# Threshold mask of an attention stage as a steep Prelu and a scaled exponential on ScalarE, with minimum pass and f16 copy on VectorE

## Chip, cores and metric

One Trainium2 chip, one core. The metric is the device time of one execution in microseconds, the median over runs; smaller is better.

## The reference

Attention with a threshold mask over 4 batches, 8 heads, 576 positions and 64 dimensions, then two gated layers on the 2304 tokens:

```python
scores = scale * np.matmul(q, k.transpose(0, 1, 3, 2))
thresh = np.max(scores, axis=-1, keepdims=True) - tau
scores = np.where(scores >= thresh, scores, -1000000000.0)
scores = scores - np.max(scores, axis=-1, keepdims=True)
attn = np.exp(scores)
attn = attn / (np.sum(attn, axis=-1, keepdims=True) + 1e-09)
x = np.matmul(attn, v)                       # then heads side by side: 2304 x 512
x = (1 / (1 + np.exp(-(x @ w_gate))) * (x @ w_val)) @ w_out
x = ((x @ w1) * (x @ w2) @ w3) @ w_out2
```

Only scores within tau (0.02) of the maximum of their row keep a weight.

## The kernel before

**Slices.** Two heads of one batch form a pair; there are 16 pairs, four to a batch. A pair is worked in nine slices of 128 rows (four for each head, and one with the last 64 rows of both heads), 144 slices in all, numbered g. A slice's scores are 128 x 576 numbers of f32 in one of two PSUM buffers (ps_s0 and ps_s1, by g odd or even).

**One slice, before.** s_mm computes the scores on TensorE. s_max (L321) takes the negated row maximum on VectorE. s_exp (L327, L328) computes the exponential into an SBUF tile e, and the threshold as a 128 x 1 column, both on ScalarE. s_mask (L336) compares the scores with the threshold, multiplies e with the outcome and adds up the row sums, on VectorE; after it the PSUM buffer is free for slice g + 2. s_hi (L344) copies e, scaled by 16384, to f16 on ScalarE. s_lo makes the rest that f16 lost, as a second f16: in the first batch and in every even slice it rescales e in place (L355 on ScalarE in the first two batches, L357 on GpSimd later) and subtracts on GpSimd (L358); in the odd slices of the other three batches one VectorE instruction (L360) does both. s_tr transposes the pair of f16 tiles by a DMA on SyncE's queue, and pv multiplies with v on TensorE five slices later.

**Order.** Engines work their own queues in order. A loop over g writes all steps; the block of s_mask, s_max, s_exp and s_mm is marked as of high priority, and a scheduler sorts all instructions by readiness in a timeline of its own and by priority. Buffers: four tiles e, four f16 tiles, five transposed ones, three of each 128 x 1 column.

**Work between.** In the first batch, TensorE multiplies w3 with w_out2 between the slices (tiles ps, th, tl, woh, wol). Later it works on the first gated layer of the batch that is finished (tiles ps_h, ps_o; 36 of its 60 units before the attention ends). Weights come as 64-bit numbers and are converted on VectorE (L450, L456), ScalarE (L455) and GpSimd (L459), then split into a high and a low part on ScalarE (L468) and GpSimd or VectorE (L469). After the attention come the rest of the first layer and the second one.

Of the kernel before, what the change touches and what calls it, by code (L numbers as in the profile page):

```python
# [8 lines left out]
F32 = mybir.dt.float32  # L9
# [13 lines left out]
def kernel(  # L23
# [33 lines left out]
    NC = S // P  # L57
    TL = S - NC * P
    NKB = NC + 1
    PSC = 16384.0  # L60

    def mm(out_, lhsT, rhs, first, last):
        nc.tensor.matmul(out_, lhsT, rhs, start=first, stop=last)  # L63
# [1 line left out]
    cst = ctx.enter_context(tc.tile_pool(name="cst", bufs=1))  # L65
# [14 lines left out]
    taub = cst.tile([P, 1], F32, name="taub")  # L80
    nc.sync.dma_start(taub, tau.partition_broadcast(P))
    zq = cst.tile([P, 1], F32, name="zq")
    nc.vector.tensor_scalar(zq, taub, 0.0, float(D) ** -0.5, op0=ALU.is_ge, op1=ALU.mult)
    ntau = cst.tile([P, 1], F32, name="ntau")
    nc.vector.tensor_scalar(ntau, taub, -1.0, None, op0=ALU.mult)
    nc.vector.tensor_tensor(ntau, ntau, taub, op=ALU.min)

    XR = cst.tile([P, KC, NT], U32, name="XR")
    XA = XR.bitcast(F32)
# [2 lines left out]
    ap_ = actx.enter_context(tc.tile_pool(name="attn", bufs=1, side="right"))  # L92
# [35 lines left out]
    prep = {}  # L128
# [126 lines left out]
    def v_scale(pr):  # L255

        vx = ap_.tile([P, 1], F32, tag="vx", name="vx")
        nc.vector.reduce_max(vx, prep[pr]["vt"], axis=AX.X)
        vp = ap_.tile([P, 1], F32, tag="vp", name="vp")
        nc.vector.tensor_single_scalar(  # L260
            vp.bitcast(I32), vx.bitcast(I32), 0x7F800000, op=ALU.bitwise_and
        )
        nc.vector.tensor_scalar(vp, vp, 2.0 ** -96, 2.0 ** 125, op0=ALU.max, op1=ALU.min)
        vs = ap_.tile([P, 1], F32, tag="vs", name="vs")
        nc.vector.reciprocal(vs, vp)
        vi = ap_.tile([P, 1], F32, tag="vi", name="vi", bufs=3)
        nc.vector.tensor_scalar(vi, vp, 1.0 / (8192.0 * PSC), None, op0=ALU.mult)
        vb = ap_.tile([P, P], BF16, tag="vb", name="vb")
        nc.scalar.activation(vb, vs.to_broadcast([P, P]), AF.Copy, scale=8192.0)
        prep[pr].update(vb=vb, vi=vi)  # L270
# [21 lines left out]
    st = {}  # L292
    NSL = 2 * NC + 1
# [22 lines left out]

    def s_max(g):
        x = st[g]
        nm = ap_.tile([P, 1], F32, tag="nm", name="nm", bufs=3)
        th = ap_.tile([P, 1], F32, tag="th", name="th", bufs=3)  # L320
        nc.vector.tensor_reduce(nm, x["ps"], axis=AX.X, op=ALU.max, negate=True)  # L321
        x.update(nm=nm, th=th)

    def s_exp(g):
        x = st[g]
        e = ap_.tile([P, S], F32, tag="e", name="e", bufs=4)
        nc.scalar.activation(e, x["ps"], AF.Exp, bias=x["nm"])  # L327
        nc.scalar.activation(x["th"], x["nm"], AF.Identity, scale=-1.0, bias=ntau)  # L328
        x["e"] = e

    def s_mask(g):
        pr, s = divmod(g, NSL)
        x = st[g]
        if s == 0:
            prep[pr]["sum"] = ap_.tile([P, NSL], F32, tag="sum", name="sum", bufs=2)
        nc.vector.scalar_tensor_tensor(  # L336
            x["e"], x["ps"], x["th"], x["e"], op0=ALU.is_ge, op1=ALU.mult,
            accum_out=prep[pr]["sum"][:, s:s + 1],
        )

    def s_hi(g):
        x = st[g]
        x["h16"] = ap_.tile([P, 2 * S], F16, tag="h16", name="h16", bufs=4)
        nc.scalar.activation(  # L344
            x["h16"][:, 0:S], x["e"], AF.Copy, scale=PSC
        )

    def s_lo(g):
        e = st[g]["e"]
        hb = st[g]["h16"]  # L350
        hi, lo = hb[:, 0:S], hb[:, S:2 * S]
        b = g // (NPAIR * NSL)
        if b == 0 or g % 2 == 0:
            if b < 2:
                nc.scalar.activation(e, e, AF.Copy, scale=PSC)  # L355
            else:
                nc.gpsimd.tensor_scalar(e, e, PSC, 1.0, op0=ALU.mult, op1=ALU.mult)  # L357
            nc.gpsimd.tensor_tensor(lo, e, hi, op=ALU.subtract)  # L358
        else:
            nc.vector.scalar_tensor_tensor(lo, e, PSC, hi, op0=ALU.mult, op1=ALU.subtract)  # L360

    def s_tr(g):
        pt = ap_.tile([P, 2 * NC + 1, P], F16, tag="pt", name="pt", bufs=5)
# [21 lines left out]
    def x_norm(pr):  # L385
        p = prep[pr]
        rs = ap_.tile([P, NSL], F32, tag="rs", name="rs", bufs=1)
        nc.vector.tensor_scalar(rs, p["sum"], 1e-9, None, op0=ALU.add)
        nc.vector.reciprocal(rs, rs)
        xn = ap_.tile([P, NC, 2, D], F32, tag="xn", name="xn")  # L390
        xt = ap_.tile([P, 2, D], F32, tag="xt", name="xt")
        nc.vector.tensor_tensor(
            xn.rearrange("p c h d -> p h c d"), p["u"],
            rs[:, 0:2 * NC].rearrange("p (h c x) -> p h c x", h=2, x=1).to_broadcast([P, 2, NC, D]),
            op=ALU.mult,
        )
# [384 lines left out]
    G = NP * NSL  # L781
# [83 lines left out]
    for g in range(G + LAG + 3):  # L865
        pr, s = divmod(g, NSL)
        steps = ahead[s] if pr + 1 < NP else ([],) * 5
        done = divmod(g - LAG, NSL)
        with tc.high_priority(offset=RING):
            if g < G:  # L870
                s_mask(g)
            if g + 1 < G:
                s_max(g + 1)
                s_exp(g + 1)
            if g + 2 < G:
                s_mm(g + 2)
# [12 lines left out]
        for f in steps[0]:
            f(pr + 1)  # L890
        for f in steps[1]:
            f(pr + 1)
        if done[1] == 2 and done[0] > 0:
            x_act(done[0] - 1)
            if done[0] % NPAIR == 0:
                xdone[0] = done[0] // NPAIR
        filler(g, 0)
        for f in steps[2]:
            if isinstance(f, str):
                if pr + 2 < NP:  # L900
# [280 lines left out]
```

## Time and profile before

| | us |
|---|---|
| median of 3 runs | 1119.43 (1118.0 to 1125.42) |
| span of the profiled execution | 1115.6 |
| TensorE (matmul) busy | 1008.3, 90% |
| VectorE busy | 774.8, 69% |
| ScalarE busy | 627.6, 56% |
| GpSimd busy | 676.3, 61% |

PE is TensorE, PEld its weight load, DVE VectorE, ACT ScalarE, POOL GpSimd, SP SyncE. L12 is line 12 of the kernel. Shares of busy time are means over stages with different limits: attention with work between it until some 673 us, gated layers afterwards. A busy TensorE is not TensorE at its peak, and the granted clock (PEclk, as a share of full speed) differs between stretches.

### The profile page before, as it was taken

Reading aid. Unit: us, or ns where it says so; the run is one execution under the profiler, and the core shown is the slowest. Engines: PE = TensorE matmul, PEld = TensorE weight load, DVE = VectorE, ACT = ScalarE, POOL = GpSimd, SP = SyncE. Lnnn points to the kernel's source line nnn. Section 1 sums busy time; section 2 is a strip of 40 time slices with the busy share of each in tenths; the row PEclk is TensorE's granted clock in tenths of the full one; section 3 lists DMA queues with packets and bytes.
Section 4 is the critical chain, followed back from the end, with each engine's and each line's share of the span. In section 5 each row is a group of like instructions: output and inputs, shape, how many; then the busy total and the mean of one; then the engine's idle time right before and its main releaser. Section 6 shows DMA issues by size and latency. Waiting matters only on the chain. (4 is left out here: it accounts for less than half of the span.)

```text
span 1115.6 us, 20323 instructions
## 1 busy us (share of the span) xinstructions
PE 1008.3 (90%) x6960; PEld 884.9 (79%) x6960; DVE 774.8 (69%) x1380; ACT 627.6 (56%) x1245; POOL 676.3 (61%) x577
## 2 busy tenths in 40 slices
PE   2598956898987999999999998999999999999997
PEld 2477845676765787777877888999999989988996
DVE  6978687888897767767877645776767644652741
ACT  4868898767777676567667644554442322331321
POOL 3755475587888586678677855677664643462530
PEclk9789967999988999999999999999999999999999
DMA  8999999999999999898988864677558826844922
GB/s 227 245 274 211 225 218 173 241 280 264 270 286 235 200 209 210 211 210 180 201 198 184 161 140 153 215 234 250 184 193 293 256 80 229 282 131 128 325 69 63
DMA packets 322422, 232.57 MB, mean 208 GB/s; under 512 B 225296, under 2 KB 253968, under 8 KB 322320
## 3 DMA queue, kind: packets, MB, share of 16 engines
q1 hardware_dynamic: 322320, 231.28, 80.9%
q8 instruction: 55, 0.90, 0.3%
q14 instruction: 47, 0.39, 0.1%
HBM read 133.17 MB, written 30.93 MB: 147 GB/s over the span
## 5 line engine op out<-in xcount | busy, mean ns | idle before, releaser
L358 POOL TENSOR_TENSOR h<-e,h 128x576 f16<-128x576 f32 x90 | 120.1, 1336 | 39.9 <-ACT e L355 29.7
L327 ACT ACTIVATE e<-ps_s,nm 128x576 f32<-128x576 f32 x144 | 106.1, 737 | 51.0 <-DVE nm L321 49.8
L336 DVE SCALAR_TENSOR_TENSOR e<-ps_s,th,e 128x576 f32<-128x576 f32 x144 | 116.2, 811 | 20.3 <-ACT th L328 12.5
L63 PEld LDWEIGHTS <-pt 128*128 128x128 f16 x2240 | 82.1, 101 | 58.8 <-DMA pt<-h 32.3
L321 DVE TENSOR_REDUCE nm<-ps_s 128x1 f32<-128x576 f32 x144 | 106.3, 751 | 28.9 <-PE ps_s L63 19.9
L344 ACT ACTIVATE h<-e 128x576 f16<-128x576 f32 x144 | 97.0, 678 | 28.3 <-DVE e L336 14.8
L63 PE MATMUL ps_s<-ka,qa 128*128 128x288 f32 x256 | 67.5, 351 | 42.2 <-DVE e L336 31.4
L63 PE MATMUL ps_h<-xl,gh 128*128 128x512 f32 (+1 forms) x240 | 94.7, 395 | 6.3 <-POOL xl L469 2.8
L63 PE MATMUL ps_h<-xl,vh 128*128 128x512 f32 (+1 forms) x240 | 92.7, 386 | 2.4 <-ACT th L685 1.3
L63 PE MATMUL ps_h<-xh,gl 128*128 128x512 f32 (+1 forms) x240 | 91.3, 380 | 3.3 <-POOL gl L469 3.3
L469 POOL TENSOR_TENSOR gl<-wg,gh 128x512 fp32r<-128x512 f32 x42 | 55.4, 1319 | 61.4 <-ACT gh L468 61.4
L63 PE MATMUL ps_y<-wm,abh 128*128 128x512 f32 x288 | 91.6, 390 | 0.2 <-DVE wm L469 0.2
L63 PE MATMUL ps_h<-xh,vl 128*128 128x512 f32 (+1 forms) x240 | 90.2, 376 | 1.6 <-POOL vl L469 1.6
L63 PE MATMUL ps_o<-gvl,oh 128*128 128x512 f32 (+1 forms) x240 | 90.4, 376 | 1.0 <-DVE XR L718 1.0
L63 PE MATMUL ps_h<-xh,gh 128*128 128x512 f32 (+1 forms) x240 | 90.8, 378 | 0.0
L63 PE MATMUL ps_h<-xh,vh 128*128 128x512 f32 (+1 forms) x240 | 90.2, 376 | 0.0
L63 PE MATMUL ps_o<-gvh,ol 128*128 128x512 f32 (+1 forms) x240 | 88.5, 369 | 0.3 <-POOL ol L469 0.3
L63 PE MATMUL ps_o<-gvh,oh 128*128 128x512 f32 (+1 forms) x240 | 88.2, 368 | 0.0
L63 PE MATMUL u<-vh,pt 128*128 128x64 f16 x640 | 62.6, 200 | 27.6 <-DMA pt<-h 27.2
L63 PEld LDWEIGHTS ps_s<-ka,qa 128*128 128x128 f32 x256 | 45.6, 210 | 50.5 <-DVE e L336 36.5
L360 DVE SCALAR_TENSOR_TENSOR h<-e,h 128x576 f16<-128x576 f32 x54 | 61.4, 1137 | 23.2 <-ACT h L344 22.8
L469 POOL TENSOR_TENSOR ol<-wo,oh 128x512 fp32r<-128x512 f32 x42 | 55.7, 1330 | 24.0 <-ACT oh L468 23.9
(198 smaller groups left out, 3025.2 us busy)
## 6 DMA issues: line engine op xcount, KB each, us to landing
wc<-sc_c SPq DMA_DIRECT2D x168, 256.0 KB, 3.2
sc_c<-wc SPq DMA_DIRECT2D x56, 256.0 KB, 2.9
XR<-in_moe_w_out_dram SPq DMA_DIRECT2D x20, 512.0 KB, 5.0
ka<-xk SPq DMA_DIRECT2D x64, 144.0 KB, 3.3
wg<-sc_g SPq DMA_DIRECT2D x36, 256.0 KB, 3.1
wv<-sc_v SPq DMA_DIRECT2D x36, 256.0 KB, 3.1
wo<-sc_o SPq DMA_DIRECT2D x36, 256.0 KB, 3.2
XR<-in_moe_w_dram SPq DMA_DIRECT2D x16, 512.0 KB, 5.0
```

Source lines behind the costliest of these rows:

```text
L63: nc.tensor.matmul(out_, lhsT, rhs, start=first, stop=last)
L321: nc.vector.tensor_reduce(nm, x["ps"], axis=AX.X, op=ALU.max, negate=True)
L327: nc.scalar.activation(e, x["ps"], AF.Exp, bias=x["nm"])
L336: nc.vector.scalar_tensor_tensor(x["e"], x["ps"], x["th"], x["e"], op0=ALU.is_ge, op1=ALU.mult, accum_out=prep[pr]["sum"][:, s:s + 1],)
L344: nc.scalar.activation(x["h16"][:, 0:S], x["e"], AF.Copy, scale=PSC)
L358: nc.gpsimd.tensor_tensor(lo, e, hi, op=ALU.subtract)
L360: nc.vector.scalar_tensor_tensor(lo, e, PSC, hi, op0=ALU.mult, op1=ALU.subtract)
L469: (lo_eng or nc.gpsimd).tensor_tensor(lo, x, hi.bitcast(F32), op=ALU.subtract)
```

## The change

q is now scaled by the negative factor, so that PSUM holds negated scores. s_max is one VectorE instruction that adds |tau| to them and accumulates the row minimum (nt, the negated threshold); its full output goes to the tile e and is overwritten later. s_exp is two ScalarE instructions: Prelu in place in PSUM, which turns the scores into score minus threshold and multiplies negative ones by 2^126, and an exponential with a bias that brings in the factor 1024 and accumulates the row sums into sum. s_mask is gone, and with it the threshold column and the rescalings. s_hi is a VectorE copy (it appears as CAST), s_lo one subtraction, on VectorE for every third slice of the last three batches (36) and on GpSimd otherwise (108). s_mm of slice g + 2 is written ahead of s_max and s_exp of slice g + 1.

```diff
-    nc.vector.tensor_scalar(zq, taub, 0.0, float(D) ** -0.5, op0=ALU.is_ge, op1=ALU.mult)
+    nc.vector.tensor_scalar(zq, taub, 0.0, -float(D) ** -0.5, op0=ALU.is_ge, op1=ALU.mult)
...
     def s_max(g):
         x = st[g]
-        nm = ap_.tile([P, 1], F32, tag="nm", name="nm", bufs=3)
-        th = ap_.tile([P, 1], F32, tag="th", name="th", bufs=3)
-        nc.vector.tensor_reduce(nm, x["ps"], axis=AX.X, op=ALU.max, negate=True)
-        x.update(nm=nm, th=th)
+        nt = ap_.tile([P, 1], F32, tag="nt", name="nt", bufs=3)
+        e = ap_.tile([P, S], F32, tag="e", name="e", bufs=4)
+        nc.vector.tensor_scalar(e, x["ps"], tauc, None, op0=ALU.add, op1=ALU.min, accum_out=nt)
+        x.update(nt=nt, e=e)
 
     def s_exp(g):
-        x = st[g]
-        e = ap_.tile([P, S], F32, tag="e", name="e", bufs=4)
-        nc.scalar.activation(e, x["ps"], AF.Exp, bias=x["nm"])
-        nc.scalar.activation(x["th"], x["nm"], AF.Identity, scale=-1.0, bias=ntau)
-        x["e"] = e
-
-    def s_mask(g):
         pr, s = divmod(g, NSL)
         x = st[g]
         if s == 0:
             prep[pr]["sum"] = ap_.tile([P, NSL], F32, tag="sum", name="sum", bufs=2)
-        nc.vector.scalar_tensor_tensor(
-            x["e"], x["ps"], x["th"], x["e"], op0=ALU.is_ge, op1=ALU.mult,
-            accum_out=prep[pr]["sum"][:, s:s + 1],
+        nc.scalar.activation(x["ps"], x["ps"], AF.Prelu, scale=-1.0, bias=x["nt"], alpha=STEEP)
+        nc.scalar.activation(
+            x["e"], x["ps"], AF.Exp, bias=ebias, accum_out=prep[pr]["sum"][:, s:s + 1]
         )
 
     def s_hi(g):
         x = st[g]
         x["h16"] = ap_.tile([P, 2 * S], F16, tag="h16", name="h16", bufs=4)
-        nc.scalar.activation(
-            x["h16"][:, 0:S], x["e"], AF.Copy, scale=PSC
-        )
+        nc.vector.tensor_copy(x["h16"][:, 0:S], x["e"])
 
     def s_lo(g):
-        e = st[g]["e"]
         hb = st[g]["h16"]
-        hi, lo = hb[:, 0:S], hb[:, S:2 * S]
-        b = g // (NPAIR * NSL)
-        if b == 0 or g % 2 == 0:
-            if b < 2:
-                nc.scalar.activation(e, e, AF.Copy, scale=PSC)
-            else:
-                nc.gpsimd.tensor_scalar(e, e, PSC, 1.0, op0=ALU.mult, op1=ALU.mult)
-            nc.gpsimd.tensor_tensor(lo, e, hi, op=ALU.subtract)
-        else:
-            nc.vector.scalar_tensor_tensor(lo, e, PSC, hi, op0=ALU.mult, op1=ALU.subtract)
+        eng = nc.vector if g >= NPAIR * NSL and g % 3 == 2 else nc.gpsimd
+        eng.tensor_tensor(hb[:, S:2 * S], st[g]["e"], hb[:, 0:S], op=ALU.subtract)
...
         with tc.high_priority(offset=RING):
-            if g < G:
-                s_mask(g)
+            if g + 2 < G:
+                s_mm(g + 2)
             if g + 1 < G:
                 s_max(g + 1)
                 s_exp(g + 1)
-            if g + 2 < G:
-                s_mm(g + 2)
```

The scheduler sorts all queues anew. On VectorE, around the end of the first batch (slices 36 to 40, shortly before the first-layer matmuls begin), the queue of before holds maximum, mask and low part (nm, e and h16 carry the numbers of their tiles; xn, yk and qbd belong to other steps):

```order
L321 TENSOR_REDUCE nm_2306<-ps_s0_88 128x1
L321 TENSOR_REDUCE nm_2343<-ps_s1_89 128x1
L336 SCALAR_TENSOR_TENSOR e_2309,sum_2341<-ps_s0_88,th_2307,e_2309 128x576
L336 SCALAR_TENSOR_TENSOR e_2346,sum_2341<-ps_s1_89,th_2344,e_2346 128x576
L321 TENSOR_REDUCE nm_2380<-ps_s0_88 128x1
L321 TENSOR_REDUCE nm_2421<-ps_s1_89 128x1
L360 SCALAR_TENSOR_TENSOR h16_2390<-e_2346,h16_2390 128x576
```

The same place on VectorE of the changed kernel, where L324 is the minimum pass and L340 the f16 copy:

```order
L324 TENSOR_SCALAR e_2207,nt_2206<-ps_s0_91,tauc_75 128x576
L324 TENSOR_SCALAR e_2241,nt_2240<-ps_s1_92,tauc_75 128x576
L340 CAST h16_2173<-e_2134 128x576
L242 TENSOR_TENSOR yk_2290<-ps_t_2344,xk_2284 128x512
L340 CAST h16_2212<-e_2169 128x576
L324 TENSOR_SCALAR e_2275,nt_2274<-ps_s0_91,tauc_75 128x576
L340 CAST h16_2245<-e_2207 128x576
L324 TENSOR_SCALAR e_2315,nt_2314<-ps_s1_92,tauc_75 128x576
```

The masks are gone from the queue, and the copies stand two to three minimum passes behind the one of their own slice. e_2275 takes the buffer of e_2134, and e_2315 that of e_2169: between the copy of a slice and the minimum pass four slices later stand two other instructions here, and the subtraction on GpSimd lies between them. In the whole queue there are 12 places where at most four instructions stand between the two and the subtraction is GpSimd's, all of them in slices 34 to 70.

ScalarE's queue of before, at the same slices, holds four instructions to a slice (xk, vh and XR belong to other steps):

```order
L344 ACTIVATE h16_2275<-e_2228 128x576
L344 ACTIVATE h16_2316<-e_2268 128x576
L355 ACTIVATE e_2228<-e_2228 128x576
L355 ACTIVATE e_2268<-e_2268 128x576
L327 ACTIVATE e_2309<-ps_s0_88,nm_2306 128x576
L328 ACTIVATE th_2307<-nm_2306,ntau_75 128x1
L327 ACTIVATE e_2346<-ps_s1_89,nm_2343 128x576
L328 ACTIVATE th_2344<-nm_2343,ntau_75 128x1
```

That of the changed kernel, with Prelu (L332) and exponential (L333):

```order
L332 ACTIVATE ps_s0_91<-ps_s0_91,nt_2206 128x576
L333 ACTIVATE e_2207,sum_2209<-ps_s0_91,ebias_79 128x576
L238 ACTIVATE xk_2284<-ps_t_2344 128x512
L332 ACTIVATE ps_s1_92<-ps_s1_92,nt_2240 128x576
L333 ACTIVATE e_2241,sum_2209<-ps_s1_92,ebias_79 128x576
L332 ACTIVATE ps_s0_91<-ps_s0_91,nt_2274 128x576
L333 ACTIVATE e_2275,sum_2209<-ps_s0_91,ebias_79 128x576
```

Two instructions a slice are left, back to back, and the second one is now the last reader of the PSUM buffer. Both queues begin with one table load and have no other.

## Rows read from the trace of the kernel before

**Rows 1.** The page: the span.

```profile
span 1115.6 us, 20323 instructions
```

**Rows 2.** Busy time by stretch: length, engines (instructions), granted clock, DMA share, GB/s.

```profile
17.00:50.00 33.00, 14.84 (x89) 12.12 (x89) 28.70 (x60) 25.17 (x50) 20.76 (x16) 0.91 1.12 251
50.00:139.00 89.00, 80.42 (x664) 68.50 (x665) 69.39 (x136) 67.78 (x132) 47.42 (x41) 0.92 1.01 239
139.00:200.00 61.00, 40.49 (x390) 34.14 (x389) 48.21 (x98) 49.64 (x101) 36.03 (x29) 0.75 0.97 196
200.00:300.00 100.00, 88.56 (x652) 71.46 (x653) 87.20 (x161) 75.90 (x149) 79.27 (x64) 0.97 1.07 268
300.00:400.00 100.00, 85.38 (x685) 70.55 (x685) 83.09 (x153) 70.98 (x142) 70.31 (x59) 0.91 1.05 238
400.00:673.00 273.00, 262.54 (x2136) 212.44 (x2134) 190.67 (x356) 178.25 (x356) 194.45 (x165) 0.99 0.86 188
673.00:1115.60 442.60, 433.68 (x2340) 414.10 (x2340) 256.77 (x394) 153.57 (x309) 224.05 (x195) 0.99 0.59 194
222.00:302.00 80.00, 72.60 (x532) 58.71 (x532) 69.73 (x127) 57.92 (x112) 68.34 (x54) 0.98 1.09 272
```

**Rows 3.** Waits, whole span: engine, line, releaser; us in total, times, longest.

```profile
PE ps_s L63 <- DVE e L336: 32.4, 19, 5.2
PE u L63 <- DMA pt<-h: 27.2, 18, 4.3
ACT h L344 <- DMA pt<-h: 11.5, 13, 2.1
```

**Rows 4.** Waits of TensorE in the first 200 us.

```profile
PE u L63 <- DMA pt<-h: 23.8, 15, 4.3
```

**Rows 5.** VectorE by line and form: count, busy us, mean ns, idle before.

```profile
L336 DVE SCALAR_TENSOR_TENSOR e<-ps_s,th,e 128x576 f32<-128x576 f32 x144 | 116.2, 811 | 20.3 <-ACT th L328 12.5 <-ACT XR L420 5.4 <-POOL h L358 1.2
L321 DVE TENSOR_REDUCE nm<-ps_s 128x1 f32<-128x576 f32 x144 | 106.3, 751 | 28.9 <-PE ps_s L63 19.9 <-PE ps_s L411 5.1 <-PE ps_s L165 2.7
L360 DVE SCALAR_TENSOR_TENSOR h<-e,h 128x576 f16<-128x576 f32 x54 | 61.4, 1137 | 23.2 <-ACT h L344 22.8
L336 DVE DVE_READ_ACCUMULATOR e<-ps_s,th,e 128x1 f32 x144 | 11.8, 82 | 0.0
L117 DVE CAST ylz<-zf 64x576 fp32r<-64x576 f32 x2 | 1.5, 747 | 1.1 <-POOL zf L112 1.1
```

**Rows 6.** The f16 tile h: shortest, median, longest ns of one.

```profile
L360 DVE SCALAR_TENSOR_TENSOR h<-e,h x54: 692/1076/3351, 184.1 to 661.2; 128x576 f16<-128x576 f32 x54
```

**Rows 7.** Timeline of GpSimd and VectorE near 209 us: start, duration.

```profile
208.91 1.28 POOL L358 TENSOR_TENSOR h<-e,h 128x576 f16<-128x576 f32 x1 [2.38 <-ACT e L355]
...
209.38 1.42 DVE L360 SCALAR_TENSOR_TENSOR h<-e,h 128x576 f16<-128x576 f32 x1
```

**Rows 8.** ScalarE by line and form.

```profile
L327 ACT ACTIVATE e<-ps_s,nm 128x576 f32<-128x576 f32 x144 | 106.1, 737 | 51.0 <-DVE nm L321 49.8
L344 ACT ACTIVATE h<-e 128x576 f16<-128x576 f32 x144 | 97.0, 678 | 28.3 <-DVE e L336 14.8 <-DMA pt<-h 11.5 <-issue 0.6
L328 ACT ACTIVATE th<-nm,ntau 128x1 f32<-128x1 f32 x144 | 41.2, 286 | 0.0
L355 ACT ACTIVATE e<-e 128x576 f32<-128x576 f32 x54 | 36.4, 678 | 0.6
```

**Rows 9.** GpSimd by line and form.

```profile
L358 POOL TENSOR_TENSOR h<-e,h 128x576 f16<-128x576 f32 x90 | 120.1, 1336 | 39.9 <-ACT e L355 29.7 <-issue 3.6 <-PE ps_s L63 1.8
L357 POOL TENSOR_SCALAR e<-e 128x576 f32<-128x576 f32 x36 | 26.1, 726 | 20.5 <-ACT h L344 20.2
```

**Rows 10.** Low parts by engine, 222 to 302 us.

```profile
L360 DVE SCALAR_TENSOR_TENSOR h<-e,h 128x576 f16<-128x576 f32 x7 | 9.5, 1360 | 0.4 <-ACT h L344 0.2
...
L358 POOL TENSOR_TENSOR h<-e,h 128x576 f16<-128x576 f32 x7 | 9.1, 1294 | 0.0
```

More of the change, by code (lines that the diff above doesn't have):

```diff
@@ L59 @@
     NKB = NC + 1
-    PSC = 16384.0
+    PSC, LN_PSC, TAU_MAX, STEEP = 1024.0, 6.931471805599453, 32.0, 2.0 ** 126
     def mm(out_, lhsT, rhs, first, last):
@@ L82 @@
     zq = cst.tile([P, 1], F32, name="zq")
-    nc.vector.tensor_scalar(zq, taub, 0.0, float(D) ** -0.5, op0=ALU.is_ge, op1=ALU.mult)
-    ntau = cst.tile([P, 1], F32, name="ntau")
-    nc.vector.tensor_scalar(ntau, taub, -1.0, None, op0=ALU.mult)
-    nc.vector.tensor_tensor(ntau, ntau, taub, op=ALU.min)
+    nc.vector.tensor_scalar(zq, taub, 0.0, -float(D) ** -0.5, op0=ALU.is_ge, op1=ALU.mult)
+    tauc = cst.tile([P, 1], F32, name="tauc")
+    nc.vector.tensor_scalar(tauc, taub, -1.0, None, op0=ALU.mult)
+    nc.vector.tensor_tensor(tauc, tauc, taub, op=ALU.max)
+    nc.vector.tensor_scalar(tauc, tauc, TAU_MAX, None, op0=ALU.min)
+    ebias = cst.tile([P, 1], F32, name="ebias")
+    nc.vector.tensor_scalar(ebias, tauc, -1.0, LN_PSC, op0=ALU.mult, op1=ALU.add)
     XR = cst.tile([P, KC, NT], U32, name="XR")
@@ L266, in v_scale @@
         vi = ap_.tile([P, 1], F32, tag="vi", name="vi", bufs=3)
-        nc.vector.tensor_scalar(vi, vp, 1.0 / (8192.0 * PSC), None, op0=ALU.mult)
+        nc.vector.tensor_scalar(vi, vp, 1.0 / 8192.0, None, op0=ALU.mult)
         vb = ap_.tile([P, P], BF16, tag="vb", name="vb")
@@ L387, in x_norm @@
         rs = ap_.tile([P, NSL], F32, tag="rs", name="rs", bufs=1)
-        nc.vector.tensor_scalar(rs, p["sum"], 1e-9, None, op0=ALU.add)
+        nc.vector.tensor_scalar(rs, p["sum"], 1e-9 * PSC, None, op0=ALU.add)
         nc.vector.reciprocal(rs, rs)
@@ L882 @@
             x_norm(done[0] - 1)
-        if g < G and g % 2 == 0 or g // (NPAIR * NSL) == 0:
+        if g < G:
             s_lo(g)
-        if 0 < g <= G and not ((g - 1) % 2 == 0 or (g - 1) // (NPAIR * NSL) == 0):
-            s_lo(g - 1)
         if 2 <= g < G + 2:
```

## The prediction

> **What bounds the kernel now.** I read the span first, then a table of stretches, then who waits for whom, then the groups of the lines that the diff touches. The profiled execution spans 1115.6 us [rows 1]; the median of the runs is 1119.43, so 3.8 us lie around the span and are added at the end.
>
> The table of stretches [rows 2] cuts the program where its work changes. From 673 us on no attention is left and TensorE is busy 433.68 of 442.6 us: nothing of the change lies there. The 144 slices of attention lie in 17 to 673 us, mixed with other matmuls. The order of instructions of the two kernels shows the same matmuls on TensorE before the last attention matmul, so the change can only remove time in which TensorE stands still or runs slowly there. Idle time is the stretch minus busy: 47 us in 17 to 200, 26 in 200 to 400, 10 in 400 to 673, in all 84. Of the clock: busy time times one minus the granted clock gives 1.3 + 6.4 + 10.1 + 2.7 + 7.7 + 2.6 = 31 us over the six stretches. The lowest clock, 0.75, stands in 139 to 200, where TensorE is also the least busy, 40.49 of 61 us.
>
> Two waits make up most of the idle time [rows 3]: the score matmuls wait for the mask (L336) to free their PSUM buffer, 32.4 us in 19 places, and the product with v waits for the transposed weights, 27.2 us in 18 places, 23.8 of them in the first 200 us [rows 4]. The other engines in the worst stretches: VectorE is busy 87.20 and 83.09 of 100 us in 200 to 400, ScalarE 49.64 of 61 us in 139 to 200, GpSimd 68.34 of 80 us in 222 to 302 [rows 2]. So TensorE is the bound late, and the chain of softmax work on three nearly full engines costs it time early.
>
> **The change part by part.**
>
> *VectorE* loses the maximum (106.3), the mask (116.2), its accumulator reads (11.8) and 54 low parts (61.4) [rows 5]: 295.7 us. It gains 144 minimum passes. That form has no row; the maximum of the same PSUM tile takes 0.751 and the mask, which also accumulates, 0.811. I take 0.78, the middle: 112.3, and 11.8 for the accumulator reads. It gains 144 casts of 128x576 from SBUF to SBUF. The one cast of that length takes 0.747 [rows 5]; the bound below is half of that, 0.374, should the cast run at double rate. I take 0.45, nearer to the double rate, because both sides are plain and contiguous, where the row's source is a repeated one. To this comes what a wait for GpSimd adds. The low part L360, whose operands all lie in SBUF, takes 1.137 on average and 0.692 at its shortest [rows 5, 6]: 0.445 more. One such case stands in [rows 7]: GpSimd runs until 210.19, VectorE's low part starts at 209.38 and ends at 210.80, 0.61 behind GpSimd. I take 0.45 + 0.445 = 0.895 a cast, 128.9 in all. The 36 low parts left cost 36 x 1.137 = 40.9. Sum added 293.9, so VectorE stays as it is (-1.8). Bounds: -97 (0.751, 0.374 without waits, 0.692) and +45 (0.811, 0.747 + 0.445, 1.137). The cast at which VectorE breaks even is (295.7 - 112.3 - 11.8 - 40.9) / 144 = 0.907 us, only just above what I take.
>
> The Trainium skill speaks against this part: "SBUF — State Buffer", section "Who interferes with whom", says that a cast within SBUF may use VectorE's second port pair, which GpSimd shares, that whoever starts first holds it for its whole instruction, and that the other stands still. By that rule each cast also holds GpSimd back, at most 144 x 0.45 = 65 us on that engine, and the time would be that of the slower rival below; were the rule not to hold, a cast would cost 0.45, VectorE would lose 66 us and the time would lie nearer to the much faster one. What [rows 7] show agrees for an instruction with two SBUF inputs; no row here shows it for a cast.
>
> *ScalarE* loses the exponential (106.1), the f16 copy (97.0), the threshold (41.2) and 54 rescalings (36.4) [rows 8]: 280.7 us. It gains Prelu in place in PSUM and an exponential with accumulator. Prelu has no row: below, the exponential's 0.737 on the same input; above, twice that, should reading and writing one bank exclude each other. I take 0.737, the row that it is nearest to. The exponential stays at 0.737. The accumulator read is bounded by VectorE's, 0.082 [rows 5], and by ScalarE's one-column instruction, 0.286; I take 0.184. Sum 106.1 + 106.1 + 26.5 = 238.7: ScalarE loses 42 us (bounds -57 and +79). In the program's order there is one table load in both kernels, so Prelu brings no others.
>
> *GpSimd* loses 36 rescalings (26.1) and goes from 90 low parts (120.1) to 108, at 1.336 each 144.3 [rows 9]: -1.9 us, but not evenly. In 222 to 302 there are 14 slices, 7 low parts on each engine [rows 10]. After the change 9.3 are on GpSimd (+2.3 x 1.294 = 3.0) and 4.7 on VectorE. If the low parts and casts on VectorE keep GpSimd waiting, the two together fill 68.3 + 3.0 + 4.7 x 0.692 + 14 x 0.45 = 80.8 of 80 us, where 68.3 + 7 x 0.692 = 73.1 do now. I count +2 us for it (0 to +7.7).
>
> *The chain.* From the end of the score matmul to the freed buffer it is now 0.751 + 0.737 + 0.286 + 0.811 = 2.585 us; afterwards 0.78 + 0.082 + 0.737 + 0.737 = 2.336, 0.25 less, with the last step on the engine that got lighter. From there to the finished f16 pair, in the slices where all is on ScalarE and GpSimd (all of the first batch), it was 0.678 + 0.678 + 1.336 = 2.69 and becomes 0.895 + 1.336 = 2.23, 0.46 less.
> - Wait for transposed weights: 27.2 / 18 = 1.51 us a time; 0.71 less is 47%: -12.8 us (0 to -27.2).
> - Wait for the score buffer: 32.4 / 19 = 1.71 a time; 0.25 less is 15%, and the release no longer stands in VectorE's queue. I take a third: -10.8 (0 to -32.4).
> - Clock: 23.6 us of 84 idle vanish; the same part of 31 would be 8.7; I take half, as many gaps stay: -4.4 (0 to -22).
>
> *Waits that move.* ScalarE's copy waits 11.5 us, 13 times, for an f16 buffer that a transposing DMA still reads [rows 3]. This wait goes to VectorE's cast, and behind it in VectorE's queue stand the next minimum passes, which start the chain. I let half reach TensorE: +5.7 (0 to +11.5). The minimum pass also writes the scratch tile e, of which there are four, so it must wait for the low part of four slices before; formerly the exponential did.
>
> Sum: -12.8 - 10.8 - 4.4 + 5.7 + 2 = -20.3. Span 1115.6 - 20.3 = 1095.3, and 3.8 around it: **1099 us**.
>
> **The rivals.**
> - *Slower: minimum passes held in VectorE's queue.* At 12 places of the new order only one to four VectorE instructions stand between the cast of a slice and the minimum pass that reuses its e, with the low part on GpSimd between them. Three of them take some 3 x 0.692 = 2.1 us; one GpSimd instruction ahead and the low part itself take 2 x 1.336 = 2.7, two ahead 4.0: a wait of 0.6 to 1.9 us, 7 to 23 us in all. With the moved 11.5 and the 2 of GpSimd this is 20 to 37 us; the minimum pass is then late, so the gains above fall away. Span 1136 to 1152, time 1140 to 1156. It decides once these holds reach TensorE with more than the 28 us of the gains. For it: GpSimd is already nearly full in 222 to 302. Against it: VectorE and GpSimd have idle time elsewhere, and most casts stand more than five rows ahead. The rule of the Trainium skill, "SBUF — State Buffer", section "Who interferes with whom", would work in its favour, by an amount that no row here shows.
> - *No change.* TensorE is the bound from 400 us on, GpSimd in 222 to 302, and what is gained in 139 to 200 is given back there: 1119 us. For it: VectorE, the fullest engine, gets no lighter.
> - *Much faster.* Both waits vanish, 59.6 us, and the clock with them, 31 x 59.6 / 84 = 22: span 1034, time 1038. Against it: the chain keeps 90% of its length. Half of that, 1079, is the most that I would expect.
> - *The change does not do what it says* is excluded: the order shows 144 casts, 144 minimum passes, and no mask, copy or rescaling.
>
> **How the numbers follow.** The forecast (a gain of 5 to 35 us) gets 0.46, much faster 0.09, no change 0.24, slower 0.21. A measurement of this kernel tells apart about 1%, 11.2 us: below 1108.2 is faster, above 1130.6 slower. Of the forecast about a sixth lies above 1108, so faster is 0.09 + 0.38 = 0.47, same 0.24 + 0.08 = 0.32, slower 0.21. The range leaves out one in ten at each end: 1066 below (a gain of 50 us, more than half of all waits), 1140 above (the near end of the slower rival). The forecast's own range is 1084 to 1114.
>
> **What would show it.** The mean of the cast: at 0.9 VectorE is as busy as before; above it, the slower rival lives. Prelu at 0.74. TensorE's wait on the score buffer should now be put down to the exponential and be near 22 us, that on transposed weights near 14. The 139 to 200 stretch should get shorter and its clock rise. I am wrong if minimum passes wait for GpSimd by over 10 us in all, if the casts wait for the DMA by more than 11.5, if Prelu takes over 1 us, or if the attention ends no earlier than 673 us although the two waits fell.

## The result

The changed kernel takes 1128.99 us (median of 10 runs, 1123.33 to 1131.3), the kernel before 1118.42 us beside it (1114.3 to 1126.07). The ratio is 1.0085, 95% interval 1.0059 to 1.0112: slower by 0.6 to 1.1%, where 1.8% faster was forecast. By the 1% that the prediction set as its bound this is the case of no change, inside the range (1066 to 1140) and outside the forecast's own (1084 to 1114). All of it lies in the attention: the first ScalarE pass over its last result starts at 682.4 us instead of 673.1, and what follows is as long as before.

The profiled execution of after spans 1124.8 us. Busy time by stretch, columns as in [rows 2]:

```profile
17.00:50.00 33.00, 16.77 (x94) 13.76 (x95) 29.71 (x60) 21.36 (x44) 21.37 (x16) 1.00 0.98 247
50.00:139.00 89.00, 80.57 (x665) 67.79 (x662) 64.90 (x136) 55.46 (x111) 45.26 (x37) 0.98 1.00 233
139.00:200.00 61.00, 38.45 (x370) 33.15 (x370) 46.74 (x100) 41.41 (x88) 40.57 (x33) 0.69 0.93 193
200.00:300.00 100.00, 84.58 (x616) 67.11 (x615) 81.03 (x146) 65.56 (x130) 73.49 (x60) 0.93 1.05 263
300.00:400.00 100.00, 84.57 (x637) 69.24 (x636) 80.26 (x143) 63.51 (x129) 75.26 (x58) 0.93 0.97 223
400.00:673.00 273.00, 264.93 (x2130) 215.16 (x2129) 182.96 (x360) 179.84 (x365) 187.47 (x146) 0.99 0.86 193
673.00:1124.80 451.80, 441.33 (x2451) 420.47 (x2449) 258.92 (x398) 157.99 (x318) 229.57 (x200) 0.99 0.60 193
```

Until 139 us the two are level (755 matmuls in 17 to 139 against 753). Then after falls behind: in 139 to 200 TensorE runs 370 matmuls where it ran 390 [rows 2], and in 200 to 300 616 where it ran 652. In 200 to 300 the other engines are all less busy too, VectorE 81.03 us instead of 87.20, ScalarE 65.56 instead of 75.90, GpSimd 73.49 instead of 79.27. So none of them became the bound there; something waits.

To the end of the attention (673.1 and 682.4 us) TensorE idles 87.3 us where it idled 83.9, and for the same 4611 matmuls it is busy 578.1 us where it was 572.2. Of the 9.3 us, 3.4 are idle time and 5.9 busy time.

The waits of after, whole span, columns as in [rows 3] (L63 is the helper that issues the matmuls):

```profile
PE ps_s L63 <- ACT e L333: 16.6, 14, 5.1
PE u L63 <- DMA pt<-h: 13.4, 9, 2.4
PE ps_s L63 <- ACT ps_s L332: 3.7, 1, 3.7
DVE h L340 <- ACT e L333: 21.6, 20, 4.2
DVE h L340 <- DMA pt<-h: 17.4, 16, 2.1
ACT ps_s L332 <- DVE e L324: 81.2, 65, 4.5
```

The score buffer now costs TensorE 16.6 + 3.7 = 20.3 us (32.4 before) and the transposed weights 13.4 (27.2). Both fell as forecast, 25.9 us together. TensorE's other waits rose: all waits together were 93.4 us in 17 to 690 us and are 97.4, so that the others went from 33.8 to 63.7. Part of what came instead stands in TensorE's waits in 60 to 400 us. Before, all waits for the preparation of the next head pair and for the norm of the last were these:

```profile
PE ps_t L156 <- DMA km<-in_k_dram: 2.4, 1, 2.4
PE ps_s L63 <- DMA ka<-xk: 1.1, 1, 1.1
PE ps_s L63 <- DVE vm L245: 1.1, 1, 1.1
PE ps_x L407 <- DVE xn L392: 0.5, 1, 0.5
PE ps_s L63 <- ACT vb L269: 0.2, 1, 0.2
```

After, in the same 60 to 400 us, the six largest are:

```profile
PE ps_s L63 <- DMA ka<-xk: 4.7, 1, 4.7
PE ps_s L63 <- DVE vx L261: 3.2, 2, 2.9
PE ps_x L392 <- DVE xn L377: 3.1, 2, 1.8
PE ps_s L63 <- DVE vnat L282: 2.9, 2, 2.7
PE ps_s L63 <- DVE vm L248: 2.3, 3, 1.3
PE ps_s L63 <- DMA ylz<-yk: 1.6, 2, 1.0
```

They add up to 17.8 us (21.1 with the smaller ones) where they were 5.3. These are short VectorE instructions (maximum vm, scale vx and product vnat of the values, norm xn), 12.9 of the 21.1 us, and the copies of the keys by DMA (ka, ylz), all steps of a pair and not of a slice. In the same stretch the score buffer and the transposed weights together fell from 33.9 to 22.0 us: 11.9 us gained, 15.8 lost.

One such place, VectorE's timeline (start, duration) and below it TensorE's:

```profile
280.51 0.68 DVE L441 SCALAR_TENSOR_TENSOR t<-XR,ps_c 128x512 uint32<-128x512 uint32 x1
281.11 0.45 DVE L340 CAST h<-e 128x576 f16<-128x576 f32 x1
281.48 0.68 DVE L377 TENSOR_TENSOR xn<-u,rs 128x512 f32<-128x512 f32 x1
282.08 1.23 DVE L345 TENSOR_TENSOR h<-e,h 128x576 f16<-128x576 f32 x1
283.23 0.28 DVE L261 TENSOR_REDUCE vx<-ps_s 128x1 f32<-128x128 f32 x1
```

```profile
279.38 0.23 PE L63 MATMUL ps_s<-identb,vm 128*128 128x128 bf16 x1
...
283.56 0.53 PE L63 MATMUL ps_s<-ka,qa 128*128 128x288 f32 x2 [2.94 <-DVE vx L261]
```

TensorE has made the input of vx at 279.6 us. VectorE takes it up at 283.23, after four instructions of other work, a cast and a low part among them. Only then may the next scores go into that buffer. By the timelines, over all 16 pairs VectorE starts vx on average 3.1 us after its input is done in before, where TensorE never waits for it, and 4.7 us in after, where it does four times.

Instructions by line and form, VectorE, ScalarE and GpSimd, columns as in [rows 5]:

```profile
L324 DVE TENSOR_SCALAR_CACHE_REDUCE e<-ps_s,tauc 128x576 f32<-128x576 f32 x144 | 115.7, 812 | 42.3 <-PE ps_s L63 27.0 <-PE ps_s L396 5.2 <-issue 3.3
L324 DVE DVE_READ_ACCUMULATOR e<-ps_s,tauc 128x1 f32 x144 | 11.7, 81 | 0.0
L340 DVE CAST h<-e 128x576 f16<-128x576 f32 x144 | 105.3, 733 | 39.6 <-ACT e L333 21.6 <-DMA pt<-h 17.4
L345 DVE TENSOR_TENSOR h<-e,h 128x576 f16<-128x576 f32 x36 | 42.4, 1179 | 0.4
L332 ACT ACTIVATE ps_s<-ps_s,nt 128x576 f32<-128x576 f32 x144 | 102.3, 712 | 82.1 <-DVE e L324 81.2
L333 ACT ACTIVATE e<-ps_s,ebias 128x576 f32<-128x576 f32 x144 | 106.6, 742 | 4.6
L333 ACT ACTIVATION_READ_ACCUMULATOR e<-ps_s,ebias 128x1 f32 x144 | 28.7, 200 | 0.0
L345 POOL TENSOR_TENSOR h<-e,h 128x576 f16<-128x576 f32 x108 | 140.4, 1302 | 110.5 <-DVE h L340 87.8 <-DVE vp L263 4.2 <-ACT ps_s L332 3.8
```

ScalarE's idle time before the exponential's chain rose from 51.0 [rows 8] to 82.1 us: it got lighter and waits for VectorE's minimum pass.

### The profile page after: what moved, and what is told of

Its sections match the earlier page's. It is cut to its first block, busy times and chain, and to the rows that moved or that the text cites. A ratio compares the mean times of both kernels' runs of the same rounds, so it can differ in the third digit from the quotient of the medians.

```text
span 1124.8 us, 20197 instructions
## 1 busy us (share of the span) xinstructions
PE 1013.6 (90%) x6960; PEld 888.3 (79%) x6960; DVE 755.7 (67%) x1364; ACT 591.6 (53%) x1191; POOL 677.0 (60%) x559
## 5 line engine op out<-in xcount | busy, mean ns | idle before, releaser
L345 POOL TENSOR_TENSOR h<-e,h 128x576 f16<-128x576 f32 x108 | 140.4, 1302 | 110.5 <-DVE h L340 87.8
L332 ACT ACTIVATE ps_s<-ps_s,nt 128x576 f32<-128x576 f32 x144 | 102.3, 712 | 82.1 <-DVE e L324 81.2
L324 DVE TENSOR_SCALAR_CACHE_REDUCE e<-ps_s,tauc 128x576 f32<-128x576 f32 x144 | 115.7, 812 | 42.3 <-PE ps_s L63 27.0
L340 DVE CAST h<-e 128x576 f16<-128x576 f32 x144 | 105.3, 733 | 39.6 <-ACT e L333 21.6
L63 PEld LDWEIGHTS <-pt 128*128 128x128 f16 x2240 | 84.1, 101 | 44.4 <-issue 20.4
L63 PE MATMUL ps_s<-ka,qa 128*128 128x288 f32 x256 | 69.5, 360 | 49.2 <-ACT e L333 16.6
L333 ACT ACTIVATE e<-ps_s,ebias 128x576 f32<-128x576 f32 x144 | 106.6, 742 | 4.6
L63 PE MATMUL ps_h<-xl,vh 128*128 128x512 f32 (+1 forms) x240 | 93.7, 390 | 5.0 <-ACT vh L453 4.2
L63 PE MATMUL ps_h<-xl,gh 128*128 128x512 f32 (+1 forms) x240 | 93.4, 389 | 4.5 <-POOL xl L454 2.8
L63 PE MATMUL ps_h<-xh,gl 128*128 128x512 f32 (+1 forms) x240 | 90.7, 378 | 3.4 <-POOL gl L454 3.4
L63 PEld LDWEIGHTS ps_s<-ka,qa 128*128 128x128 f32 x256 | 46.2, 215 | 59.1 <-ACT e L333 20.1
L63 PE MATMUL ps_h<-xh,vl 128*128 128x512 f32 (+1 forms) x240 | 90.5, 377 | 2.0 <-POOL vl L454 2.0
L63 PE MATMUL ps_y<-wm,abh 128*128 128x512 f32 x288 | 91.4, 390 | 0.3 <-DVE wm L454 0.3
L63 PE MATMUL ps_o<-gvl,oh 128*128 128x512 f32 (+1 forms) x240 | 90.5, 377 | 1.0 <-DVE XR L703 1.0
L63 PE MATMUL ps_h<-xh,gh 128*128 128x512 f32 (+1 forms) x240 | 90.4, 376 | 0.0
L63 PE MATMUL ps_h<-xh,vh 128*128 128x512 f32 (+1 forms) x240 | 89.5, 373 | 0.0
L63 PE MATMUL ps_o<-gvh,oh 128*128 128x512 f32 (+1 forms) x240 | 88.8, 371 | 0.0
L63 PE MATMUL ps_o<-gvh,ol 128*128 128x512 f32 (+1 forms) x240 | 88.8, 370 | 0.0
L63 PE MATMUL u<-vh,pt 128*128 128x64 f16 x640 | 62.9, 200 | 13.6 <-DMA pt<-h 13.4
L454 POOL TENSOR_TENSOR gvl<-gr,gvh 128x512 fp32r<-128x512 f32 (+1 forms) x48 | 64.7, 1347 | 12.3 <-ACT gvh L453 12.3
```

Source lines behind the costliest of these rows:

```text
L324: nc.vector.tensor_scalar(e, x["ps"], tauc, None, op0=ALU.add, op1=ALU.min, accum_out=nt)
L332: nc.scalar.activation(x["ps"], x["ps"], AF.Prelu, scale=-1.0, bias=x["nt"], alpha=STEEP)
L333: nc.scalar.activation(x["e"], x["ps"], AF.Exp, bias=ebias, accum_out=prep[pr]["sum"][:, s:s + 1])
L340: nc.vector.tensor_copy(x["h16"][:, 0:S], x["e"])
L345: eng.tensor_tensor(hb[:, S:2 * S], st[g]["e"], hb[:, 0:S], op=ALU.subtract)
L454: (lo_eng or nc.gpsimd).tensor_tensor(lo, x, hi.bitcast(F32), op=ALU.subtract)
```

## The experiments

Each time is a median, each ratio is to the kernel before on the same chip, with its 95% interval. The runs fall into three rounds of questions.

### Which part of the change is it

The cast (L340) is held up by GpSimd, as the timeline of after shows near 235 and 241 us:

```profile
234.93 1.26 POOL L454 TENSOR_TENSOR vl<-wv,vh 128x512 fp32r<-128x512 f32 x1
235.17 1.33 DVE L340 CAST h<-e 128x576 f16<-128x576 f32 x1
...
241.35 1.30 POOL L454 TENSOR_TENSOR gl<-wg,gh 128x512 fp32r<-128x512 f32 x1
241.54 1.43 DVE L340 CAST h<-e 128x576 f16<-128x576 f32 x1
```

The casts end 0.31 and 0.32 us after the GpSimd instruction that had started before them; an undisturbed one takes 0.444. Three theories followed: A, the new order of the queues; B, casts and GpSimd hold each other; C, the minimum pass waits for the low part through the four tiles e.

**mm_last** writes the scores of g + 2 behind s_exp again.

```
-            if g + 2 < G:
-                s_mm(g + 2)
             if g + 1 < G:
                 s_max(g + 1)
                 s_exp(g + 1)
+            if g + 2 < G:
+                s_mm(g + 2)
```

> The changed kernel with one thing undone: s_mm of slice g + 2 is written behind s_max and s_exp of slice g + 1 again, as in the kernel before. No instruction is added or taken away; only the order that the scheduler builds can differ. Theory A (order: the 10 us are lost between slices 48 and 60 because the queues' new order does not fit the real durations, so each engine stands behind instructions that are not ready): the slip at slices 48 to 60 changes by several us, to either side; between 1112 and 1140. Theory B (port: casts and GpSimd hold each other up in 215 to 295 us): as the changed kernel, 1125 to 1133. Theory C (ring: the minimum pass waits for the low part of four slices before through e): as the changed kernel, 1125 to 1133.

**lo_half** puts every second low part of the last three batches on VectorE, as before (`g % 2 == 1` for `g % 3 == 2`).

> The changed kernel with the low parts shared out as before: in the last three batches every second slice on VectorE (54 in all), 90 on GpSimd. In 215 to 295 us GpSimd gets about two instructions fewer (2.6 us), VectorE two more of 1.2. Theory B (port and a full GpSimd): the slip at slices 48 to 60 shrinks by 2 to 5 us, 1121 to 1127. Theory A (order): changed by several us to either side. Theory C (ring): fewer minimum passes wait for GpSimd, 1122 to 1128.

**scratch** lets the minimum pass write its full output to an f16 tile of its own; e is taken in s_exp.

> The changed kernel with the full output of the minimum pass in a tile of its own (f16, never read), so that e is taken only by the exponential, as before. The minimum pass no longer waits for the low part of four slices before. Theory C (ring): the slip at slices 48 to 60 is gone, 1113 to 1121. Theory B (port): as the changed kernel, 1125 to 1133. Theory A (order): the scheduler is free to place minimum passes earlier; changed by several us to either side.

**copy_act** makes the f16 copy on ScalarE.

```
-        nc.vector.tensor_copy(x["h16"][:, 0:S], x["e"])
+        nc.scalar.activation(x["h16"][:, 0:S], x["e"], AF.Copy)
```

> The changed kernel with the f16 copy on ScalarE (a plain Copy) and not on VectorE. VectorE loses 144 casts of 733 ns (105 us), ScalarE gains 144 of about 680 ns (98 us). Theory B (port): the slip is gone, 1112 to 1121, GpSimd instructions over 1.35 us become rare. Theory A (order): ScalarE gets fuller, the order is another one; no particular sign, 1115 to 1140. Theory C (ring): the low part starts no earlier, so the same, 1125 to 1133.

Measured: mm_last 1128.38 us (1.0090, 1.0062 to 1.0118), lo_half 1125.05 (1.0073, 1.0044 to 1.0103), scratch 1129.26 (1.0088, 1.0062 to 1.0114), copy_act 1117.66 (0.9987, 0.9968 to 1.0005). The place of s_mm, the split of the low parts and the tiles e are not the cause (1125.05 lies in the ranges of B and C for lo_half, but the interval of its ratio holds the 1.0085 of after); the minimum pass waits for the low part on GpSimd 0.8 us in all in after. The copy matters: on ScalarE it takes away 11 us.

### Port, place or time

**noport** keeps the copy on VectorE in a form with an accumulator.

```
-        nc.vector.tensor_copy(x["h16"][:, 0:S], x["e"])
+        nc.vector.tensor_scalar(
+            x["h16"][:, 0:S], x["e"], 1.0, 0.0, op0=ALU.mult, op1=ALU.add, accum_out=ej
+        )
```

> The f16 copy stays on VectorE at its place in the queue, but as a tensor_scalar with an accumulator (x1.0 + 0.0), a form like the min pass, which takes 0.81 us plus a 0.08 us read everywhere in the trace of after and is never seen stretched (the cast takes 444 ns at the least, 733 in the mean, 992 in 215 to 295 us). Theory PORT (the casts and GpSimd's passes hold each other between 215 and 295 us): no copy above 0.85 us, GpSimd's passes no longer held, the 10 us slip at slices 48 to 60 is gone, 1117 to 1121 us. Theory TIME (it is the VectorE time of 0.7 to 1.0 us a slice that is missing, whatever holds it): the copy costs 0.83 + 0.08 = 0.91 us in the mean against 0.733, 144 x 0.18 = 25 us more of VectorE, so slower than after: 1129 to 1138 us. Theory QUEUE (the copy stands in VectorE's queue behind the exponential and holds up what is behind it): as after, 1126 to 1131 us.

Measured 1134.7 us (1.0137, 1.0114 to 1.0159). The copies by tile, shortest, median and longest in ns, of after and then of noport:

```profile
L340 DVE CAST h<-e x144: 444/462/1546, 21.9 to 668.4; 128x576 f16<-128x576 f32 x144
```

```profile
L341 DVE TENSOR_SCALAR_CACHE_REDUCE h<-e x144: 685/746/755, 22.2 to 673.8; 128x576 f16<-128x576 f32 x144
```

The form with the accumulator is never held. It is still slower than after: with its reads it takes 118.7 us of VectorE instead of 105.3. So the hold is real, some (733 - 462) ns x 144 = 39 us, but taking it away gains nothing. That the time on VectorE is what counts instead fits this run; it is not shown by it alone, as the order is another one too. The Trainium skill, "SBUF — State Buffer", section "Who interferes with whom", says that cast and tensor_scalar can use the second port pair, but not the form that writes out its accumulator; these two rows agree.

**act_b1** and **dve_b1** put the copy on ScalarE in the second batch only, and, for dve_b1, everywhere but there (`36 <= g < 72`, and `not`), because the slices of after slip against before in that batch: the exponential of slice 48 ends 2.2 us earlier than in before, that of slice 60 11.6 us later.

> The f16 copy goes to ScalarE for slices 36 to 71 (the second batch, which contains the slip at slices 48 to 60) and stays on VectorE for the other 108. If the loss of after sits in that batch's stretch alone (219 to 282 us): 1117 to 1119 us, or up to 2 us less if the copies on VectorE gain elsewhere. If the loss merely shows there and the cast costs time throughout: 1122 to 1127 us.

> The complement: the f16 copy on ScalarE for 108 slices, on VectorE only for slices 36 to 71. If the loss sits in that batch alone: 1127 to 1130 us as after. If it is spread over all slices: 1118 to 1122 us.

Measured 1125.25 us (1.0065, 1.0033 to 1.0097) and 1126.42 (1.0064, 1.0037 to 1.0091). act_b1 lies in the range for a cost throughout, dve_b1 in neither of its two. Each half costs most of the whole, so the place where the slip shows is not the only one where it is caused.

**before_cast** is the kernel before with its f16 copy on VectorE.

> The kernel before with one edit: the f16 copy (here with the factor 16384) by VectorE instead of ScalarE, mask and scaling passes kept. It adds a pass of 0.45 to 1.0 us a slice to VectorE, which in 215 to 285 us is busy 62.5 of 70 us with 14 slices in it. Theory PORT or TIME: +7 to +14 us in that stretch or more, since here nothing is taken away from VectorE: 1128 to 1150 us. If the copy on VectorE costs only beside the min pass with its accumulator (that is, if it is not the copy alone): 1117 to 1122 us.

Measured 1145.27 us (1.0229, 1.0208 to 1.0250). The copy takes 118.7 us of VectorE there, and TensorE's wait for the mask rises from 32.4 to 53.9 us. Here the copy alone was moved, though the scheduler draws a new order with it.

### Is it the order

Halves that don't add up made me doubt the order that the scheduler draws. **before_ring60**, **before_ring130** and their counterparts change one number, RING (90), by which the scores and the steps of the softmax are drawn ahead. **prep_hi** puts the preparation of the next pair under the same priority, **before_prep_hi** does so in the kernel before.

```
+        with tc.high_priority(offset=RING):
             for f in steps[3]:
                 f(pr + 1, g)
             if done[1] == 0 and done[0] > 0:
                 x_norm(done[0] - 1)
...
+        with tc.high_priority(offset=RING):
             for f in steps[0]:
                 f(pr + 1)
             for f in steps[1]:
                 f(pr + 1)
```

> The kernel before with the one number RING at 60 instead of 90: how far ahead the scheduler draws the score, maximum and exponential steps of a slice. No work changes, only the written order of all engines. Theory LUCK (the orders that the scheduler makes differ by several us, and before has a good one): 1123 to 1130 us. Theory WORK (after is slower because of what its steps cost, not because of the order drawn): 1115 to 1121 us. Four orders of after (it, and mm_last, lo_half, scratch) lie at 1125 to 1129 us.

> The same with RING at 130. LUCK: 1123 to 1130 us. WORK: 1115 to 1121 us.

> After, with the preparation of the next head pair (its steps on ScalarE, VectorE and TensorE) and the norm of the pair that ends written inside the same priority that draws the scores ahead. In 60 to 400 us TensorE's waits for the preparation and the norm (maximum, scale and product of the values, norm, duplicated keys) are 21.1 us in after and 5.3 in before, while its waits for the score buffer and the transposed weights fell from 33.9 to 22.0. Theory PREP (these waits took the place of those removed and are a loss of their own): they fall below 12 us and the time to 1118 to 1123 us. Theory TIME (VectorE is what is late, and the wait is only named by what comes last): the preparation waits fall, others rise, and the time stays at 1125 to 1130 us.

> The control of prep_hi: the same edit in the kernel before, whose TensorE waits only 5.3 us for the preparation. PREP and WORK: 1116 to 1121 us. LUCK: anywhere from 1116 to 1130 us.

> After with RING at 60 instead of 90; before at 60 took 1123.1 us. Theory ORDER (the change's work is worth nothing or a gain, after at 90 had an order that happens to be bad beside one of before that happens to be good): 1112 to 1123 us, at or under before at 60. Theory WORK (the cast in VectorE's queue costs 5 us and more in any order): 1127 to 1134 us.

> The same at 130, where before took 1126.3 us. ORDER: 1114 to 1126 us. WORK: 1130 to 1137 us.

> copy_act (f16 copy on ScalarE) with RING at 60. If the -11 us of copy_act against after is its work: 1115 to 1121 us, well under after at 60. If it was the order it drew at 90: within 3 us of after at 60.

> The same at 130: work: 1115 to 1121 us, well under after at 130; order: within 3 us of after at 130.

Measured, us, with the ratio to the kernel before at 90:

| order | before | after | copy_act |
|---|---|---|---|
| RING 60 | 1123.12, 1.0047 (1.0017 to 1.0076) | 1128.66, 1.0096 (1.0076 to 1.0116) | 1119.31, 1.0024 (1.0007 to 1.0041) |
| RING 90 | 1 | 1128.99, 1.0085 (1.0059 to 1.0112) | 1117.66, 0.9987 (0.9968 to 1.0005) |
| RING 130 | 1126.31, 1.0074 (1.0047 to 1.0100) | 1127.56, 1.0098 (1.0070 to 1.0126) | 1114.17, 0.9972 (0.9954 to 0.9990) |
| prep_hi | 1127.39, 1.0090 (1.0061 to 1.0119) | 1133.9, 1.0128 (1.0089 to 1.0168) | - |

before_prep_hi is the kernel before in the row prep_hi. Two things follow. The kernel before has a good order at 90: the other three, with the same work, are 0.5 to 0.9% slower. And the copy on VectorE costs 0.7, 1.0 and 1.3% against the copy on ScalarE, in all three orders, some 11 us. After against before in the same order is +0.5, +0.85, +0.2 and +0.4%, on average 0.5% or 5.5 us. In RING 130 and prep_hi the intervals of the two overlap, so as an estimate about half of the result is the change and the rest the good order that the kernel before had. prep_hi did not shorten the preparation waits as hoped (19.4 us in 60 to 400 against 21.1), so it does not tell whether they are a loss of their own.

Other runs tell more of these waits. The largest of copy_act in 60 to 400 us:

```profile
PE ps_s L63 <- DMA ylz<-yk: 3.3, 1, 3.3
PE ps_s L63 <- DVE vm L248: 3.1, 3, 1.7
PE ps_s L63 <- DVE vx L261: 3.0, 2, 2.8
PE ps_s L63 <- DVE vnat L282: 2.2, 2, 1.7
```

Counted as for after they are 17.1 us, and all waits of TensorE in 17 to 690 are 94.1, though VectorE is 100 us less busy in the attention than before. In noport, slower than after, they are 11.1; in the four orders of the kernel before 4.1 to 7.4. So these waits came with the change, wherever its copy runs, and they are not what the 11 us of the copy consist of. Against copy_act, the attention of after is 8.6 us longer: 5.8 us of busy and 2.8 of idle TensorE.

How an order alone costs time is seen in the stretches, of before at 90 and then at 60 (columns as in [rows 2]; the attention ends at 673.1 and 679 us):

```profile
17.00:215.00 198.00, 150.21 (x1258) 126.88 (x1259) 158.54 (x316) 155.32 (x308) 112.48 (x92) 0.87 1.01 226
215.00:400.00 185.00, 159.48 (x1225) 129.88 (x1222) 158.04 (x290) 134.15 (x263) 141.31 (x115) 0.94 1.07 256
```

```profile
17.00:215.00 198.00, 148.65 (x1197) 125.80 (x1198) 150.91 (x304) 149.69 (x296) 109.32 (x89) 0.84 0.95 219
215.00:400.00 185.00, 160.72 (x1235) 131.53 (x1232) 161.18 (x292) 132.56 (x261) 138.91 (x111) 0.92 1.05 254
400.00:679.00 279.00, 269.23 (x2192) 217.81 (x2188) 196.49 (x369) 184.67 (x372) 200.22 (x170) 1.00 0.89 192
```

TensorE's idle time to the end of the attention is the same, 83.9 and 83.4 us. Its busy time for the same matmuls is 572.2 and 578.6, and the granted clock fell from 0.87 and 0.94 to 0.84 and 0.92. By the prediction's sum (busy time times one minus the granted clock, the stretch from 400 us on included) 36.6 us are lost to the clock where it was 31.7: an estimate, as a clock is given in hundredths, but most of the 6 us. What in the order lowered the clock is not shown. copy_act has 572.3 us busy and 84.5 idle.

**act_pass_e** and **act_pass_const** leave the copy on ScalarE and add a pass to VectorE that nobody reads, of the exponential or of a constant.

```
         nc.scalar.activation(x["h16"][:, 0:S], x["e"], AF.Copy)
+        nc.vector.tensor_copy(ej, x["e"])
```

> copy_act (1117.7 us) with one more pass a slice: VectorE copies the same exponential to an f16 tile that nobody reads, as after's cast, with its wait for the exponential. Theory QUEUE or TIME (what stands in VectorE's queue is late, whoever reads the copy): 1125 to 1132 us as after. Theory CONSUMER (the f16 copy itself comes later from VectorE, and with it low part, transpose and product): 1116 to 1121 us.

> copy_act with a VectorE copy of the same size (576 columns, f32 to f16) of a constant, which waits for nothing and which nobody reads. TIME (0.4 to 0.75 us a slice of VectorE are enough): 1124 to 1132 us. QUEUE (it is the wait for the exponential in front of the next minimum pass): 1116 to 1121 us, while act_pass_e is slow.

Measured 1140.66 us (1.0164, 1.0114 to 1.0215) and 1145.61 (1.0204, 1.0161 to 1.0248), where the kernel before took 1123.33. A pass that nobody reads costs 1.8% over copy_act, some 20 us, so the theory that the readers of the copy get it late falls. Both times lie above every range that had been named. From act_pass_e to after the copy leaves ScalarE and its readers take VectorE's: 1.0164 to 1.0085, some 9 us gained. Twenty lost and nine gained make the 11; each kernel has an order of its own here, so each of these may be off by the few us that the table shows.

act_pass_const was to tell time from the wait for the exponential. The scheduler drew its passes ahead; here are their busy time and count on VectorE by stretch, then the stretch for all engines in that run:

```profile
17.00:139.00 122.00, 51.11 (x71) 0.94 0.92 223
139.00:215.00 76.00, 43.57 (x60) 0.66 0.74 164
215.00:400.00 185.00, 0.00 (x0) 0.94 1.02 250
```

```profile
17.00:215.00 198.00, 129.09 (x1008) 109.41 (x1008) 192.28 (x360) 129.63 (x257) 107.74 (x83) 0.83 0.85 200
```

VectorE is full there, 192.28 of 198 us, and TensorE idles 68.9 us against 46.1 in copy_act; the attention ends 24.2 us later. So 95 us of VectorE time without any wait cost about a quarter of themselves in this order. It does not show what they would cost if they were spread like the casts.

## Why the prediction was wrong

- **VectorE's sum: prices nearly right, conclusion wrong.** The minimum pass took 0.812 us (0.78 forecast) and its read 0.081. The cast took 0.462 in the middle and 0.733 on average where 0.45 + 0.445 was forecast: the base was right, the wait for GpSimd 0.27 instead of 0.445. VectorE as a whole got 19 us lighter (774.8 to 755.7), not 1.8, and still the kernel is slower. Busy time was the wrong measure here: the casts wait 39.6 us at the head of VectorE's queue, and steps of a pair come late (vx by 4.7 us instead of 3.1). That the first causes the second is not shown: in copy_act, without casts on VectorE, vx comes 4.6 us late.
- **ScalarE: right.** Prelu 0.712, exponential 0.742, read 0.200 (0.737, 0.737, 0.184 forecast), together 237.6 us against 238.7. But the time freed there was worth only some 9 us for a 97 us copy (act_pass_e to after).
- **GpSimd: right and without weight.** Low parts 140.4 us (144.3), in all 677.0 (676.3 before). In 222 to 302 it is busy 63.87 us, less than the 68.34 before, so the +2 us counted for it did not arise.
- **The two waits: right in size.** 20.3 and 13.4 us against 21.6 and 14.4 forecast.
- **The failed step: taking these 23.6 us as time gained.** The prediction asked what the two waits would shrink to and not what TensorE would meet next; for TensorE's other waits its sum had nothing but half of the moved wait (+5.7). They rose from 33.8 to 63.7 us, the preparation of the next pair among them from 5.3 to 21.1 in 60 to 400, and all waits of TensorE together went from 93.4 to 97.4 us in 17 to 690. In copy_act it is 94.1, so this step fails wherever the copy runs.
- **The clock: no time came back.** 4.4 us were to. 139 to 200 went from 0.75 to 0.69, but 17 to 50 from 0.91 to 1.00; by the prediction's own sum over the six stretches 28 us are lost where it was 31. Still TensorE was busy 5.9 us longer with the same matmuls. That sum does not explain it, nor does another number here.
- **The moved wait: too small.** 11.5 us on ScalarE became 17.4 on VectorE, beyond the bound that the prediction had named, with 21.6 for the exponential on top, which had no term in the sum. Two of the four signs of being wrong came true: this one, and an attention that ends later than 673 us although the two waits fell.
- **The base: not questioned.** The sum started from one order of the kernel before. Three others of it are 5 to 9 us longer, so a change that redraws the order could lose some of that. No trace of before alone could have told; it took other orders of it.
- **The slower rival** had the right sign and the wrong mechanism: minimum passes wait for GpSimd 0.8 us, not 7 to 23. What it takes from the Trainium skill, "SBUF — State Buffer", section "Who interferes with whom", is seen in the trace (0.444 to 1.546 us a cast). The price of it is not: noport, without it, is no faster.
- **The rival of no change** has the right class by the wrong way: nothing was gained in 139 to 200 that could be given back in 222 to 302, and VectorE did get lighter.

What stays open: by which way the copy on VectorE costs its 11 us; why TensorE is busy 5.9 us longer than before; why the rest of the change (mask to Prelu, threshold and rescalings gone) gains only 0.1 to 1.0% with the copy on ScalarE, though VectorE loses about 100 us by it in the attention (507 to 405 in 17 to 673); and whether the preparation waits are a loss of their own or other lateness under another name.

The best version measured is act_ring130, the change with the copy on ScalarE and RING 130: 1114.17 us, 0.28% under the kernel before (0.10 to 0.46%), the lowest of the three orders tried.

## What to carry to other kernels

When a wait of the bounding engine is shortened, look up what that engine meets next and on whose queue that stands: here 25.9 us gained in two waits became 4 us more in all. An engine's free time is not the price of a pass moved onto it: here one more pass cost some 20 us on VectorE, busy 60% of the span in copy_act, and the same pass taken from ScalarE gave back some 9. Compare the new waits with those of a variant of another speed before calling them the cause: here they were nearly as long in the faster kernel. Where a scheduler draws the order, time a few orders of the kernel before as well, as one of them may be 0.5 to 0.9% better than its neighbours by luck.

## What the runs showed of the hardware

- In after a cast of 128x576 from f32 to f16 within SBUF takes 0.444 us at the least and up to 1.546 beside GpSimd; the same copy as a tensor_scalar with accumulator takes 0.685 to 0.755 and is never held.
- ScalarE's accumulator read takes 0.200 us after each exponential, VectorE's 0.081.
- Prelu in place in PSUM (0.712 us) is no slower than an exponential from PSUM to SBUF (0.742).
- The same matmuls kept TensorE busy for 572 or 578 us, by the order of the work around them alone, with the idle time unchanged (before at RING 90 and 60; granted clock 0.87 and 0.94 against 0.84 and 0.92 in the two stretches).
